# Four weight pieces, eight first taps and one transposition placed elsewhere in a fused attention and MoE kernel

## The chip, the core and the metric

The kernel runs on one core of a Trainium2 chip. A core has five engines that follow their own instruction streams in order: TensorE (PE, matmuls and its weight loads PEld), VectorE (DVE), ScalarE (ACT), GpSimd (POOL) and SyncE (SP), which here issues nearly all transfers between the chip's main memory and SBUF. The metric is the device time of one launch in microseconds.

## The reference, cut to what matters

Attention with rotated q and k (4 batches, 8 heads, 576 tokens, 64 values a head), and behind it a gated layer with a convolution of three taps over the tokens:

```python
scores = scale * np.matmul(rotate(q), rotate(k).transpose(0, 1, 3, 2))
attn = softmax(scores)
x = np.matmul(attn, v)                      # heads side by side: 4 x 576 x 512
h = np.maximum(x @ w_in, 0.0)               # 512 -> 1024
conv_out[:, s] = sum(conv_w[t] * h[:, s + t - 1] for t in range(3))
gate = 1.0 / (1.0 + np.exp(-conv_out))
out = h * gate @ w_out                      # 1024 -> 512
```

## The kernel before

**Steps.** The 32 heads are taken as 16 pairs p, each cut in five row tiles s. One tile is one step, so there are 80 steps n = 5p + s. In a step PE makes the scores of a tile (L261, 4 products in 8 instructions), DVE takes the negated row maxima (L269), ACT the exponentials (L273), and one step later PE turns the result (L321, a leftover part in L358) and ACT copies it to the tile pt (L199). When a pair's five tiles are there, PE multiplies by v in two halves (emit_E, L389), and DVE makes reciprocals of the sums (emit_rinv, L366 to L368), which go by SP through main memory and come back as rb (L371 to L376).

**The second layer.** From step WIDE = 26 on the PSUM pools change and the layer's work is laid into the steps beside attention. Of a block of 288 tokens, unit f (one of eight slices of 128 hidden values) is a call of emit_M1: twelve matmuls (L428), ACT's ReLU into rr (L436), and a chain that is spread over the next steps: conv (DVE: first tap L440, two more taps L442), tanh (ACT, L448), gate (DVE, L451), split (ACT copy L459, then POOL's subtraction L460). The first block's units 0 to 7 are in steps 26, 27, 28, 29, 31, 32, 33 and 34, one each; from step 36 on there are two units in a step, or half a row tile of the second product (L531, from step 37).

**The weights.** They are 64-bit numbers, converted in sixteen pieces of 128 x 512. A piece has five parts: ACT's absolute value into wt (L557), on DVE a clamp (L560), a shift (L566), the low bits (L571) and the result into wf (L576). When the last part is written out the next but one load into w64 is issued on SP (L596). One step later, at rank 0.12, ACT rounds wf into the high half (L626) and POOL subtracts, in four instructions, for the low half (L623). The last four pieces, 12 to 15 in the list (here W0 to W3, the last rows of w_out), live in the pool wl with one buffer of wt and one of wf, and their parts are placed by the table LATEW.

**Order.** The order is written out by hand: `at(n, rank, fn)` puts work in step n at a rank, all engines' streams are filled in rising step and rank, and each engine runs its own stream in that order; only semaphores hold an instruction back. Ranks around the change, from step 26 on: split and tanh 0.1, rounding of a piece 0.12, maxima 0.2, conv and gate of the first block 0.3, the transposition of q or k (emit_TQ, L234 and L237, L243) 0.45, turns 1, exponentials 1.5, copies to pt 1.6, a unit 2, weight parts 2.6, the leftover's copy 5 (11 in step 26), emit_E 10, rotation on POOL (rope, six L190 and three L193) 18, load of v 19, loads of q and k (six transfers each, L149 to L151) 19.6. Raw q and raw k have one buffer each: a load waits for the transposition of the pair before, and the rotation for the load. Pairs that concern us: pair 6 (k transposed in step 28), pair 7 (loads in step 26, rotation in 27 and 28, transposition in 30), pair 8 (loads in step 30, rotation in 32 and 33, transposition in 35).

Of the kernel before, what the change touches and what calls it, by code (L numbers as in the profile page):

```python
# [11 lines left out]
AF = mybir.ActivationFunctionType  # L12
ALU = mybir.AluOpType
# [7 lines left out]
def attention_moe_kernel(ctx, tc, q, k, v, w_in, conv_w, w_out, tab, tabx, out):  # L21
    nc = tc.nc
# [7 lines left out]
    HS = S // 2  # L30
# [5 lines left out]
    scale = float(D) ** -0.5  # L36
# [24 lines left out]
    cw = keep.tile([128, 32], F32, name="cw")  # L61
# [13 lines left out]
    late = {"tail": False, "u": 0}  # L75
# [5 lines left out]
    def defer(k, fn, rank=1):  # L81
        due.setdefault(slot[0] + k, []).append((rank, len(due.get(slot[0] + k, [])), fn))
# [30 lines left out]
    def m_tile():  # L113
        if late["tail"]:
            return psum["t"].tile([128, 512], F32, tag="mt", name="mt")
        ps = m_pair()
        pair["k"] ^= 1
        return ps[1 - pair["k"]]
# [86 lines left out]
    def qk_tiles(p):  # L205
        if p not in QT:
            QT[p] = p2.tile([128, S], F32, tag="qT", name="qT")
            KT[p] = p2.tile([128, S + 64], F32, tag="kT", name="kT")
# [21 lines left out]
    def emit_TQ(p, part):  # L230
        qk_tiles(p)
        x = raw.pop((p, part))[:, :, 0, :]
        if part == "q":
            nc.vector.transpose(out=QT[p].rearrange("p (c i) -> p c i", i=32), in_=x)  # L234
        else:
            kt = KT[p].rearrange("p (c i) -> p c i", i=32)
            nc.vector.transpose(out=kt[:, 2:20], in_=x)  # L237
            if p * STEPS < WIDE:
                for h in range(2):
                    r = slice(64 * h, 64 * h + 64)  # L240
                    nc.vector.transpose(out=krem[p % 2][r, r].rearrange("p (c i) -> p c i", i=32), in_=x[r, 16:18])
            if p * STEPS + STEPS > WIDE:
                nc.vector.transpose(out=kt[:, 0:2], in_=x[:, 16:18])  # L243
# [174 lines left out]
    def emit_M1(blk, f, last=False):  # L418
        b, j = divmod(blk, 2)
        g, rr = late["g"], late["rr"]  # L420
        ps = m_tile()
        fs = slice(128 * f, 128 * f + 128)
        n = 3 * NK
        i = 0
        for kk in range(NK):
            xs = xslot[b, kk, j]
            for w, e in ((winh, 0), (winh, 1), (winl, 0)):
                nc.tensor.matmul(  # L428
                    out=ps[:, 0:XW], lhsT=w[:, kk, fs], rhs=xT[:, xs, e, :], start=(i == 0), stop=(i == n - 1)
                )  # L430
                i += 1
        if f == NF - 1:
            for kk in range(NK):
                free_slots.append(xslot.pop((b, kk, j)))
        r = rr[(blk * NF + f) % len(rr)]
        nc.scalar.activation(out=r[:, 1:XW], in_=ps[:, j:j + XW - 1], func=AF.Relu, scale=0.5)  # L436
        c = late["pc"].tile([128, HS], F32, tag="c", name="c")

        def conv():
            nc.vector.tensor_scalar(out=c, in0=r[:, j:j + HS], scalar1=cw[:, f:f + 1], scalar2=None, op0=ALU.mult)  # L440
            for e in (1, 2):
                nc.vector.scalar_tensor_tensor(  # L442
                    out=c, in0=r[:, j + e:j + e + HS], scalar=cw[:, 8 * e + f:8 * e + f + 1], in1=c,
                    op0=ALU.mult, op1=ALU.add,
                )

        def tanh():
            nc.scalar.activation(out=c, in_=c, func=AF.Tanh)  # L448

        def gate():  # L450
            nc.vector.scalar_tensor_tensor(  # L451
                out=c, in0=c, scalar=1.0, in1=r[:, j + 1:j + 1 + HS], op0=ALU.add, op1=ALU.mult
            )

        def split():
            o = 0
            for dst, n in g_pieces(blk, f):
                hi, lo = dst[:, 0, :], dst[:, 1, :]
                nc.scalar.activation(out=hi, in_=c[:, o:o + n], func=AF.Copy)  # L459
                nc.gpsimd.tensor_tensor(out=lo, in0=c[:, o:o + n], in1=hi.bitcast(F32), op=ALU.subtract)  # L460
                o += n
            ready.add((blk, f))

        if late["tail"]:
            for k, fn in enumerate((conv, tanh, gate, split)):
                defer(k + 1, fn)
        else:
            n = late["n"] + last
            for k, rank, fn in ((0, 0.3 if last else 2.5, conv), (1, 0.1, tanh), (2 - last, 0.3, gate), (3 - last, 0.1, split)):
                at(n + k, rank, fn)  # L470

# [3 lines left out]
    def g_pieces(blk, f):  # L475
        res, tok = [], blk * HS
        end = tok + HS
        while tok < end:
            if tok >= TAIL:
                n = end - tok  # L480
                res.append((late["ga"][:, f, :, tok - TAIL:end - TAIL], n))
            else:
                pos = tok % RING
                k = pos // RA
                n = min(end - tok, (RING if k else RA) - pos, TAIL - tok)
                assert all(t < 0 or t in done_tt for t in ((tok - RING) // 128, (tok + n - 1 - RING) // 128))
                res.append((late["g"][k][:, :, f, pos - RA * k:pos - RA * k + n], n))
            tok += n
        return res
# [178 lines left out]
    for i in range(WEARLY):  # L668
# [3 lines left out]
    WIDE = 26  # L672
# [2 lines left out]
    HALVES = [37, 39, 42, 44, 47, 49, 52, 54, 57, 59, 62, 64, 67, 68, 72, 73, 76, 78]  # L675
    NORM = {4: 8}
    LATEW = (
# [4 lines left out]
    )  # L682
    plan = {}
    onpe = (0, 0.2, 0.5, 1, 2, 2.4, 3, 4, 10)
# [2 lines left out]
    def at(n, rank, fn):  # L687
        plan.setdefault(n, []).append((rank, len(plan.get(n, [])), fn))

    def emit():  # L690
        with tc.manual_schedule(engines=engines):
# [17 lines left out]
            for p in range(1, NP):  # L709
                n = STEPS * p  # L710
                early = n - 10 >= WIDE - 1
                for i, part in enumerate("qk"):
                    if p > 1:
                        at(max(n - 10, WIDE) if early else n - 9 + 2 * i, 19.6 if early else 19, lambda p=p, part=part: load(p, part))
                    at(n - 8 + i if early else max(n - 6 + i, 0) if p > 1 else 0, 18, lambda p=p, part=part: rope(p, part))
                    at(n - 5 if early else max(n - 4 + 2 * i, 2), 0.45, lambda p=p, part=part: emit_TQ(p, part))
                at(n + 1, 19, lambda p=p: load_v(p))
            for p in range(NP):
                n = STEPS * p
# [36 lines left out]
            for n, k in UNITS.items():  # L756
                for i in range(k):
                    blk, f = divmod(late["u"], NF)
                    late["u"] += 1
                    at(n, 2 + 0.4 * i, lambda blk=blk, f=f, last=i == k - 1: emit_M1(blk, f, last))  # L760
# [3 lines left out]
            n = -1  # L764
# [96 lines left out]
```

## Time and profile before

| what | value |
| --- | --- |
| median of 3 runs | 497.78 us (494.35 to 498.48) |
| the profiled execution | 498.89 us, its span 496.9 us |
| mean granted TensorE clock | 0.983 |
| busy PE, PEld | 456.6 us (92%), 360.1 us (72%) |
| busy DVE, ACT, POOL | 364.1 us (73%), 329.2 us (66%), 301.5 us (61%) |
| chain that ended last | PE 69%, DVE 11%, SP's queue 7%, DMA 6%, ACT 4% |

The span runs from the first to the last instruction; 1.99 us of the profiled execution lie outside it. Shares of busy time are means over stages that have different limits, so they are read by stage. In the rows further on, a number in brackets at a row's end is the time for which the engine stood idle in front of it, and behind the arrow stands what ended that wait.

### The profile page before, as it was taken

To read this page: it belongs to the slowest core of one execution; us is meant where nothing else is said; L and a number is where in the kernel's file an instruction comes from. 1 tells how busy PE (TensorE), PEld (TensorE's weight loads), DVE (VectorE), ACT (ScalarE), POOL (GpSimd) and SP (SyncE) were. 2 spreads that over 40 slices of the span, in tenths; PEclk is the share of its full clock that TensorE was granted. 3 is DMA by queue.
4 is the path that set the end of the run, shared out by engine and by line. 5 is a ranking of instruction groups with operands and counts; after the bars stand their busy time and mean duration, and the time that the engine had idled before them with its cause. 6 is when DMAs were issued, how large, how long until landed. Compare 5 with 4: busy or idle time off the path is not lost.

```text
span 496.9 us, 12411 instructions
## 1 busy us (share of the span) xinstructions
PE 456.6 (92%) x4572; PEld 360.1 (72%) x4572; DVE 364.1 (73%) x644; ACT 329.2 (66%) x943; POOL 301.5 (61%) x495
## 2 busy tenths in 40 slices
PE   1869889888687999999999999999999999999997
PEld 1336456555565779797978787979797878899886
DVE  5587897898798988686868687777674665567921
ACT  2678887796476768696868686868687763244510
POOL 3598979999378975848584849393921213234520
PEclk9999989999799899999999999999999999999999
DMA  8986787547542507080807090707120200100011
GB/s 225 149 162 156 152 163 167 116 93 162 114 92 63 82 14 143 14 154 17 151 29 139 14 154 12 141 27 128 41 60 13 60 13 25 42 23 22 0 58 48
DMA packets 140559, 42.71 MB, mean 86 GB/s; under 512 B 132156, under 2 KB 135252, under 8 KB 140500
## 3 DMA queue, kind: packets, MB, share of 16 engines
q1 hardware_dynamic: 139156, 41.54, 40.5%
q8 instruction: 36, 0.59, 0.5%
q10 hardware_dynamic: 1344, 0.39, 0.4%
q14 instruction: 23, 0.19, 0.1%
HBM read 37.12 MB, written 4.79 MB: 84 GB/s over the span
## 4 chain that ended last, share of the span: by engine, by line
PE 69%; DVE 11%; SPq 7%; DMA 6%; ACT 4%; issue 2%; POOL 1%; DVEq 0%; POOLq 0%; ACTq 0%
PE pm L428 13%; PE sp L261 12%; PE pm L531 10%; PE mt L511 10%; PE pm L389 10%; PE mt L428 7%; PE tp L321 5%; SPq L150 3%; DVE negm L269 2%; DMA rk<-k 2%; DVE wt L560 2%; ACT st L273 2%; DMA vm<-v 2%; SPq L151 1%; SPq L149 1%
## 5 line engine op out<-in xcount | busy, mean ns | idle before, releaser
L269 DVE TENSOR_REDUCE negm<-sp 128x1 f32<-128x576 f32 x144 | 102.6, 748 | 36.2 <-PE sp L261 21.9
L273 ACT ACTIVATE st<-sp,negm 128x576 f32<-128x576 f32 x128 | 94.0, 742 | 31.6 <-DVE negm L269 30.8
L261 PE MATMUL sp<-kT,qT 64*128 64x288 f32 (+4 forms) x556 | 103.1, 469 | 5.4 <-ACT st L273 3.0
L199 ACT ACTIVATE pt<-tp 128x512 f32<-128x512 f32 (+3 forms) x176 | 84.1, 530 | 4.8 <-PE tp L321 4.3
L442 DVE SCALAR_TENSOR_TENSOR c<-rr,cw,c 128x288 f32<-128x288 f32 x128 | 79.4, 620 | 4.5
L460 POOL TENSOR_TENSOR gm<-c,gm 128x288 fp32r<-128x288 f32 (+4 forms) x72 | 45.1, 631 | 55.3 <-ACT gm L459 55.1
L428 PE MATMUL pm<-xT,winh 128*128 128x290 f32 x352 | 76.0, 310 | 0.0
L190 POOL TENSOR_TENSOR rq<-rq,tabt 128x192 f32<-128x192 f32 x90 | 59.3, 693 | 17.9 <-DMA rq<-q 17.7
L261 PEld LDWEIGHTS sp<-kT,qT 64*128 64x128 f32 (+1 forms) x556 | 48.1, 179 | 27.5 <-issue 8.8
L410 POOL TENSOR_TENSOR xT<-xn,xT 128x290 fp32r<-128x290 f32 x32 | 28.0, 876 | 59.3 <-ACT xT L406 58.3
L321 PEld LDWEIGHTS tp<-idf,st 64*128 64x128 f32 x1024 | 43.3, 140 | 25.7 <-ACT st L273 15.4
L190 POOL TENSOR_TENSOR rk<-rk,tabt 128x192 f32<-128x192 f32 x90 | 57.4, 671 | 2.9 <-DMA rk<-k 2.9
L428 PEld LDWEIGHTS pm<-xT,winh 128*128 128x128 f32 x352 | 57.4, 193 | 1.9
L321 PE MATMUL tp<-idf,st 64*128 64x64 f32 x1024 | 48.8, 228 | 10.8 <-ACT st L273 10.6
L428 PE MATMUL pm<-xT,winl 128*128 128x290 f32 x176 | 52.7, 299 | 0.0
L389 PE MATMUL pm<-pt,vm 128*64 128x290 f32 x368 | 50.1, 411 | 2.4 <-ACT pt L199 2.4
L531 PE MATMUL pm<-wouth,gm 64*128 64x256 f32 x512 | 49.3, 282 | 0.0
L440 DVE TENSOR_SCALAR c<-rr,cw 128x288 f32<-128x288 f32 x64 | 29.1, 455 | 22.1 <-ACT rr L436 19.3
L451 DVE SCALAR_TENSOR_TENSOR c<-c,rr 128x288 f32<-128x288 f32 x64 | 36.4, 590 | 9.4 <-ACT c L448 9.4
L531 PEld LDWEIGHTS pm<-wouth,gm 64*128 64x128 f32 x512 | 43.0, 185 | 0.0
L389 PEld LDWEIGHTS pm<-pt,vm 128*64 128x64 f32 x368 | 25.8, 136 | 19.8 <-ACT pt L199 3.5
L531 PE MATMUL pm<-woutl,gm 64*128 64x256 f32 x256 | 38.9, 276 | 0.0
(118 smaller groups left out, 909.8 us busy)
## 6 DMA issues: line engine op xcount, KB each, us to landing
rq<-q SPq DMA_DIRECT2D x30, 144.0 KB
rq<-q SPq DMA_DIRECT2D x60, 72.0 KB
rk<-k SPq DMA_DIRECT2D x30, 144.0 KB
rk<-k SPq DMA_DIRECT2D x60, 72.0 KB
w<-moe_w_in SPq DMA_DIRECT2D x8, 512.0 KB
vm<-v SPq DMA_DIRECT2D x32, 128.0 KB
w<-moe_w_out SPq DMA_DIRECT2D x8, 512.0 KB
rb<-rd SPq DMA_DIRECT2D x16, 144.0 KB
```

Source lines behind the costliest of these rows:

```text
L190: nc.gpsimd.tensor_tensor(out=y, in0=y, in1=tabt[:, a:a + 3], op=ALU.mult)
L199: nc.scalar.activation(out=out, in_=in_, func=AF.Copy, scale=1.0 if sc is None else sc)
L261: nc.tensor.matmul(out=out, lhsT=qt[64 * h:64 * h + 64, c], rhs=kt[64 * h:64 * h + 64, a:a + n], start=True, stop=True)
L269: reds.setdefault((p, s), []).append(lambda: nc.vector.tensor_reduce(out=nm, in_=sc, axis=AX.XY if len(sc.shape) == 3 else AX.X, op=ALU.ma ...
L273: lambda: nc.scalar.activation(out=dst, in_=sc, func=AF.Exp, bias=nm, scale=1.0, accum_out=sm)
L321: nc.tensor.transpose(ps[r][:, 64 * k:64 * k + 64], x[i], idf[i, i])
L389: nc.tensor.matmul(out=xp[64 * h:64 * h + 64, :], lhsT=vmain[p][:, h, i, :] if i < 4 else vrem[p % 2][:, h, :], rhs=pt[:, 2 * i + h if i < ...
L428: nc.tensor.matmul(out=ps[:, 0:XW], lhsT=w[:, kk, fs], rhs=xT[:, xs, e, :], start=(i == 0), stop=(i == n - 1))
L442: nc.vector.scalar_tensor_tensor(out=c, in0=r[:, j + e:j + e + HS], scalar=cw[:, 8 * e + f:8 * e + f + 1], in1=c, op0=ALU.mult, op1=ALU.add,)
L460: nc.gpsimd.tensor_tensor(out=lo, in0=c[:, o:o + n], in1=hi.bitcast(F32), op=ALU.subtract)
L511: nc.tensor.matmul(out=ops[tt][:, 0:width], lhsT=g_tile(tt, f, e), rhs=w[:, f, cols], start=(f == 0 and i == 0), stop=(f == NF - 1 and i = ...
L531: nc.tensor.matmul(out=ps[r][:, 0:256], lhsT=g_tile(tt, f, e)[rows], rhs=w[rows, f, cols], start=(f == 0 and i == 0), stop=(f == NF - 1 an ...
```

## The change

Three edits. The first tap of the first block's eight units goes from DVE to ACT and from the step after the unit into the unit's own step (rank 5.2). The table LATEW gets other steps: W0 is cut in halves over steps 26 and 27, W1 over 29 and 31, W2 over 32 and 33, W3 stays whole in 34. The transposition of k of pair 7 goes from step 30 to 31.

```diff
+        def tap():
+            nc.scalar.activation(out=c, in_=r[:, j:j + HS], func=AF.Copy, scale=cw[:, f:f + 1])
+
         def conv():
-            nc.vector.tensor_scalar(out=c, in0=r[:, j:j + HS], scalar1=cw[:, f:f + 1], scalar2=None, op0=ALU.mult)
+            if blk:
+                nc.vector.tensor_scalar(out=c, in0=r[:, j:j + HS], scalar1=cw[:, f:f + 1], scalar2=None, op0=ALU.mult)
             for e in (1, 2):
...
             n = late["n"] + last
+            if not blk:
+                at(late["n"], 5.2, tap)
...
     LATEW = (
-        ((25, 0.4), (26, 2.6), (26, 2.6), (26, 2.6), (26, 2.6)),
-        ((26, 5.5), (27, 2.6), (27, 2.6), (29, 2.6), (29, 2.6)),
-        ((29, 5.5), (31, 2.6), (31, 2.6), (31, 2.6), (31, 2.6)),
-        ((31, 5.5), (33, 2.6), (33, 2.6), (34, 2.6), (34, 2.6)),
+        ((25, 0.4), (26, 2.6), (26, 2.6), (27, 2.6), (27, 2.6)),
+        ((27, 5.5), (29, 2.6), (29, 2.6), (31, 2.6), (31, 2.6)),
+        ((31, 5.5), (32, 2.6), (32, 2.6), (33, 2.6), (33, 2.6)),
+        ((33, 5.5), (34, 2.6), (34, 2.6), (34, 2.6), (34, 2.6)),
     )
...
-                    at(n - 5 if early else max(n - 4 + 2 * i, 2), 0.45, lambda p=p, part=part: emit_TQ(p, part))
+                    at(n - 5 + i * (n - 10 < WIDE) if early else max(n - 4 + 2 * i, 2), 0.45, lambda p=p, part=part: emit_TQ(p, part))
```

## Rows read from the trace of the kernel before

**Rows 1.** The page's slices: PE's busy tenths in 40 slices of the span.

```profile
PE   1869889888687999999999999999999999999997
```

**Rows 2.** Stretches, steps 26 to 30: busy us of each engine, PEclk, DMA share, GB/s.

```profile
117.90:128.10 10.20, 7.08 (x76) 5.08 (x73) 10.06 (x8) 3.20 (x9) 8.07 (x23) 1.00 0.19 64
128.10:135.20 7.10, 5.87 (x30) 4.84 (x32) 3.98 (x9) 5.10 (x15) 2.50 (x4) 0.52 0.88 195
135.20:140.40 5.20, 5.20 (x63) 4.26 (x58) 5.13 (x10) 3.72 (x11) 3.58 (x6) 1.00 0.07 5
140.40:145.40 5.00, 4.87 (x41) 3.23 (x41) 4.83 (x9) 3.04 (x9) 2.45 (x4) 1.00 0.67 121
145.40:153.40 8.00, 6.79 (x64) 4.70 (x61) 6.41 (x13) 5.81 (x16) 7.67 (x12) 1.00 0.22 67
```

**Rows 3.** Timeline of DVE, steps 26 to 34: start, us, instruction, idle before it.

```profile
119.97 6.29 DVE L560 TENSOR_SCALAR wt<-wt 128x512 f32<-128x512 f32 x1
126.75 0.69 DVE L571 SCALAR_TENSOR_TENSOR wt<-w,wt 128x512 int32<-128x512 int32 x1
127.48 0.69 DVE L576 SCALAR_TENSOR_TENSOR wf<-w,wt 128x512 int32<-128x512 int32 x1
...
135.19 1.42 DVE L269 TENSOR_REDUCE negm<-sp 128x1 f32<-128x576 f32 x2 [3.02 <-PE sp L261]
...
136.89 0.71 DVE L440 TENSOR_SCALAR c<-rr,cw 128x288 f32<-128x288 f32 x1
...
151.49 0.78 DVE L237 STREAM_TRANSPOSE kT<-rk 128x576 f32<-128x576 f32 x1 [1.45 <-POOL rk L193]
...
174.41 0.90 DVE L576 SCALAR_TENSOR_TENSOR wf<-w,wt 128x512 int32<-128x512 int32 x1
```

**Rows 4.** DVE's clamp and shift by line: durations in ns, least, median, most.

```profile
L560 DVE TENSOR_SCALAR wt<-wt x17: 404/591/6293, 19.9 to 167.3; 128x512 f32<-128x512 f32 x16, 32x128 f32<-32x128 f32 x1
L566 DVE TENSOR_SCALAR wt<-wt x17: 414/569/1045, 22.3 to 168.2; 128x512 int32<-128x512 int32 x16, 32x128 int32<-32x128 int32 x1
```

**Rows 5.** Timeline of ACT: the wait in step 26, a split, the wait in 35.

```profile
128.21 0.66 ACT L557 ACTIVATE wt<-w 128x512 f32<-128x512 f32 x1 [6.65 <-DVE wf L576]
...
138.94 0.49 ACT L459 ACTIVATE gm<-c 128x288 fp32r<-128x288 f32 x1
...
175.34 0.63 ACT L626 ACTIVATE wouth<-wf 128x512 fp32r<-128x512 f32 x1 [1.50 <-DVE wf L576]
```

**Rows 6.** Timeline of PE: the first work of step 27, and emit_E's second half.

```profile
129.33 0.48 PE L358 MATMUL pm<-idf,st 64*128 64x64 f32 x2 [4.35 <-ACT pt L199]
...
176.35 2.20 PE L389 MATMUL pm<-pt,vm 128*64 128x290 f32 x15 [1.01 <-ACT pt L199]
```

**Rows 7.** Timeline of SP: issues in steps 30 and 31.

```profile
153.54 1.36 SPq L371 DMA_DIRECT2D rd<-rt  x4
...
160.48 0.50 SPq L151 DMA_DIRECT2D rq<-q  x1
...
164.69 0.50 SPq L151 DMA_DIRECT2D rk<-k  x1
```

**Rows 8.** Timeline of POOL: rotations in steps 25, 32 and 33, and what surrounds them.

```profile
120.72 3.35 POOL L190 TENSOR_TENSOR rk<-rk,tabt 128x192 f32<-128x192 f32 x6
124.03 1.68 POOL L193 TENSOR_TENSOR rk<-rk 128x192 f32<-128x192 f32 x3
...
160.71 2.40 POOL L623 TENSOR_TENSOR woutl<-wf,wouth 128x128 fp32r<-128x128 f32 x4
163.76 4.08 POOL L190 TENSOR_TENSOR rq<-rq,tabt 128x192 f32<-128x192 f32 x6 [0.65 <-DMA rq<-q]
...
170.81 4.95 POOL L190 TENSOR_TENSOR rk<-rk,tabt 128x192 f32<-128x192 f32 x6
175.72 1.90 POOL L193 TENSOR_TENSOR rk<-rk 128x192 f32<-128x192 f32 x3
177.58 0.86 POOL L460 TENSOR_TENSOR gm<-c,gm 128x288 fp32r<-128x288 f32 x1
```

## The prediction, made before the changed kernel ran

> **What bounds the kernel now.** I read the page's slices first: from about the fifteenth slice on PE shows nines nearly to the end, before that sixes to eights [rows 1]. So a microsecond saved in the later steps off PE is worth nothing, and one by which PE's unbroken stretch starts sooner is worth a whole one. The change lies just ahead of that stretch, in steps 26 to 36, and the question is when PE gets its first work after which it never waits again. The timeline of PE gives that point: the second half of emit_E in step 35, at 176.35, for which it stood idle 1.01 us [rows 6]. That wait ends with a copy by ACT, which stood behind the rounding L626 of the last weight piece W3, which waited for DVE's L576 of W3, started at 174.41 [rows 3, 5]. So **the start of L576 of W3 sets the end of this stage**, and I follow how it gets there.
>
> Then I read the stretches by step. In steps 28 and 29 DVE is busy 5.13 of 5.20 and 4.83 of 5.00 us; it is the bound there [rows 2]. Steps 26, 27 and 30 are longer for other reasons. In step 26 (10.20 us) one clamp of W0 took 6.29 us where the median is 0.59 [rows 3, 4]; meanwhile POOL rotated k of pair 6 without a pause, 120.72 to 125.7 [rows 8]. In step 27 (7.10 us) DVE is busy 3.98 us and waits 3.02 for scores [rows 2, 3]: ACT had stood 6.65 us in front of L557 of W1, which needs the buffer that L576 of W0 reads [rows 5]; with ACT's copies held, PE was idle 4.35 us [rows 6], and after that it ran at a granted clock of 0.52 in the stretch, the lower of its two levels, 1.2 instead of 2.4 GHz [rows 2]. In step 30 (8.00 us) DVE waits 1.45 us at the transposition of k of pair 7 for POOL's rotation [rows 2, 3].
>
> **The change, step 26 to step 30.** Up to the clamp in step 26 all streams are the same, so I keep its 6.29 us. Behind it L571 and L576 of W0, 0.69 us each [rows 3], go to step 27: 1.4 us gained. In step 27 L557 of W1 now stands at the very end, so ACT's copies in step 26 are free, PE goes on without the 4.35 us and without the slow clock. What then sets step 27 is DVE: 3.98, less a tap of some 0.7 (0.71 one step later) and less the clamp and shift of W1 (medians 0.59 and 0.57), plus 1.38, is 3.5 [rows 2, 3, 4]; ACT has as much to do, so I take 4.0 of the 7.10: 3.1 gained. If PE gives its slow clock to these steps all the same, this falls to some 1. Step 28 loses the tap: 0.7. Step 29 loses the tap and exchanges two parts of a piece for two others; but PE was busy 4.87 of its 5.00 us [rows 2], so I count 0.4, not 0.9. In step 30 DVE's 6.41 lose the tap, 0.7, and the 0.78 of k's transposition, and the wait of 1.45 goes: some 4.9. PE's 6.79 of that step [rows 2] are a limit only so far as PE has not begun ahead of DVE, and it has, since maxima wait for nothing there; I take 5.0 of 8.00, 3.0 gained (1.2, if PE's 6.79 rule). Sum at the end of step 30: 1.4 + 3.1 + 0.7 + 0.4 + 3.0 = **8.6 us**, with 5 to 9 as ends.
>
> The tap itself costs ACT eight instructions like the split's copy of the same shape, 0.49 us at most [rows 5], before some overlap; 0.4 a step. ACT has gaps of over a microsecond in each step (busy 3.04 of 5.00, 3.72 of 5.20, 5.81 of 8.00 [rows 2]). If they were full it would cost up to 0.49 a step, 3.9 in all; it is held in the ends. It needs no wait but the ReLU ahead of it on the same engine. The transposition of k in step 31 lets the load of raw k of pair 8, issued in step 30, start only then; on SP the next behind it are the load of W3 and v. The rotation needs that k late, so this costs nothing.
>
> **The change, step 31 to step 35.** Here an order turns round. wf has one buffer. L576 of W3 may write it only when POOL's four L623 of W2 have read it. Before, W2 was finished in step 31, its L623 ran at 160.71, ahead of POOL's two rotations of pair 8 [rows 8]. Now W2 is finished in step 33 and its L623 are in POOL's stream in step 34, behind both rotations (steps 32 and 33) and behind one L460. And the rotations can't start sooner than raw q of pair 8 has landed, which SP loads only after the reciprocals' trip of step 30. I count from the issue of that trip, 153.54 before [rows 7]: to the rotation's start at 163.76 it is 10.2 us (the last load of q is issued at 160.48); from there to the start of the second rotation at 170.81 7.05; the second took 6.77, to 177.58 [rows 8]. When DVE stands still a rotation takes 3.35 + 1.68 = 5.03 [rows 8]; DVE will stand still in its last third, so 6.1. L460 0.85. The L623 took 2.40 with DVE at work [rows 8], 2.0 by the same ratio as L190 (3.35 to 4.08). L576 itself 0.69 [rows 3]. Together 26.9 us. Before, L576 of W3 ended at 174.41 + 0.90, that is 21.8 after the trip's issue. So **5.1 of the 8.6 us are given back to a new wait of DVE for POOL**, and 3.5 are left. Behind the waiting L576 on DVE stand the maxima of step 35, and on ACT L626 of W3 and the copies that emit_E needs. The bounds: both rotations at 5.03 gives 2.8 given back; both at the slowest rows (4.95 + 1.90) and L623 at 2.40 gives 6.1 [rows 8].
>
> That wait has a second price. PE can do the first half of emit_E, but then idles several microseconds before the second. After 4.35 us of idling its granted clock was 0.52 over 7.10 us, with PE busy 5.87 [rows 2, 6]. There it cost little beyond the step; here every later microsecond of PE counts, so a spell like it would cost up to 2.9 (half of 5.87). It can also fall into the idle time itself, and cost nothing. I take 2.0. Net gain 3.5 - 2.0 = 1.5. The profiled execution took 498.89, so 497.4; the median run lies 1.1 below the profiled one, so **496.3 us**.
>
> W3's load is now behind the twelve loads of pair 8 on SP, whose last is issued 11.2 us after the trip (164.69) [rows 7]. W3's first part on ACT comes at about 15 us after it; if the piece lands later, ACT and DVE wait, but DVE waits for POOL then anyway, so nothing is added up to some 4 us of lateness.
>
> **The rivals.** (a) *The wait on POOL is short and PE keeps its clock*: rotations near 5.03, gain 8.6 - 2.8 = 5.8, **492.0**. For it: fewer taps on DVE beside the rotations; against: DVE works through the whole first rotation. (b) *No wait on POOL at all*, the whole 8.6: **489.2**. It would take q landing 3 us sooner or more; no row shows that. (c) *The clamp's 6.29 us do not come again*. Then DVE's maxima of step 27 can begin at 125 (PE ended there, 129.33 - 4.35) instead of 126.7, 1.8 sooner: **494.5** [rows 3, 6]. For it: only one of 17 clamps shows it [rows 4]; against: nothing ahead of it is changed. The Trainium skill, page "SBUF — State Buffer", section "SBUF: two separate sides", says that VectorE and GpSimd share a port pair as an exclusive lock, held for one instruction by whichever starts first. By that the clamp would wait for one POOL instruction, some 0.6 us, and this rival would be the rule; the trace does not agree, since the 6.29 us span all nine instructions of a rotation. (d) *The gain of the first steps does not come*: PE's 6.79 rule step 30, slow clock in steps 27 and 28, taps fill ACT: 8.6 becomes 5, less 5.1, no further clock price: **497.9**, no change. (e) *Slower*: one more clamp is caught by a rotation as that of step 26 was. W3's clamp now stands in step 34, beside the second rotation, and W1's in step 29 beside that of pair 7's k. One costs 6.29 - 0.59 = 5.7 us of DVE where DVE rules: **502.0**. It decides from a stall of 1.5 us on.
>
> **How the numbers follow.** The forecast 0.42 (own range 494 to 498.5), (a) 0.16, (b) 0.07, (c) 0.13, (d) 0.14, (e) 0.08. About one per cent, 5 us, is what a measurement of this kernel tells from no change. Below 492.8 are (b), most of (a), a little of (c): 0.20. Above 502.8 is part of (e) and a little of (d): 0.05. Within: 0.75. The range 490.5 to 501.0 leaves out (b), most of (e) and the ends of the others.
>
> **What would show each step right or wrong.** In the changed profile: L557 of W1 no longer with a wait of over 6 us, PE's idle time ahead of step 27 gone, and a granted clock of 1.0 from 128 to 135; the reciprocals of step 30 end near 145; no wait at k's transposition of pair 7. Then L576 of W3 on DVE with a wait of 3 to 6 us for POOL's L623, PE idle 3 us or more ahead of emit_E's second half, near 172.9, and a stretch at about half clock behind it. If that L576 has no wait, (b) holds. If the clamp of step 26 is short, (c). If the reciprocals end after 149, the first sum is wrong. A clamp of over 2 us in steps 29 to 34 is (e).

## The result, and the profile after

The changed kernel takes 499.81 us, median of its runs (497.61 to 508.68); the kernel before, timed beside it on the same chip, takes 496.44 us (492.88 to 502.08). The ratio is 1.0077, with a 95% interval of 1.0047 to 1.0106: it is slower by 0.8%. The ratios here and below are formed from the fast runs alone, those within 1.5% of the fastest of their kernel, so they are not the quotients of the medians beside them, and of a kernel with two lengths a part of the longer executions is left out (12 of 29 where the kernel before has a median of 497.89). The forecast was 496.3 us, a little under the median of 497.78 that was known for the kernel before. The time lies within the range of 490.5 to 501.0 and within the 1% that was called no change, but the small effect has the other sign.

| | before | after |
|---|---|---|
| median, us | 496.44 | 499.81 |
| profiled execution, us | 498.89 | 500.04 |
| its span, us | 496.9 | 498.2 |

In the changed file the lines behind the new function stand six lower: the tap on ACT is L440, the conversion's clamp L566, its result L582, the rounding L632, POOL's subtraction L629, the zeros at the borders of rr L784 and L785.

I go through the profile by the points that the prediction named. First the stretches of steps 26 to 30, which answer to [rows 2]; the columns are the same: busy us of PE, PEld, DVE, ACT and POOL, the granted clock as a share of 2.4 GHz, DMA share, GB/s.

```profile
120.67:128.78 8.11, 7.05 (x76) 5.05 (x71) 8.07 (x5) 4.03 (x13) 7.45 (x22) 1.00 0.31 78
128.78:132.42 3.64, 3.50 (x30) 3.13 (x32) 3.57 (x7) 3.06 (x11) 0.00 (x0) 1.00 0.89 156
132.42:137.52 5.10, 4.41 (x55) 3.27 (x50) 4.94 (x9) 5.10 (x16) 4.24 (x7) 1.00 0.00 0
137.52:142.12 4.60, 4.60 (x45) 3.77 (x43) 4.29 (x8) 4.60 (x15) 4.36 (x7) 1.00 0.86 160
142.12:147.36 5.24, 5.24 (x50) 3.14 (x48) 4.74 (x10) 4.20 (x13) 4.38 (x7) 1.00 0.20 77
...
172.90:179.70 6.80, 3.53 (x15) 3.27 (x17) 5.81 (x9) 3.30 (x9) 5.01 (x9) 0.52 0.01 2
```

Steps 26 to 30 together take 26.69 us instead of 35.50. The clock is full in all five of them, as forecast. The last row is behind them: from 172.9 on PE runs at the lower level, 1.2 GHz, which the trace of before does not show there. The timeline of DVE (start, us, instruction, the idle time before it and its releaser) tells why:

```profile
120.67 1.42 DVE L269 TENSOR_REDUCE negm<-sp 128x1 f32<-128x576 f32 x2 [1.87 <-PE sp L261]
...
122.70 5.71 DVE L566 TENSOR_SCALAR wt<-wt 128x512 f32<-128x512 f32 x1
...
147.36 1.42 DVE L269 TENSOR_REDUCE negm<-sp 128x1 f32<-128x576 f32 x2 [0.40 <-PE sp L261]
...
149.64 0.76 DVE L237 STREAM_TRANSPOSE kT<-rk 128x576 f32<-128x576 f32 x1
...
173.85 1.27 DVE L582 SCALAR_TENSOR_TENSOR wf<-w,wt 128x512 int32<-128x512 int32 x1 [4.52 <-POOL woutl L629]
...
201.22 1.42 DVE L269 TENSOR_REDUCE negm<-sp 128x1 f32<-128x576 f32 x2
```

L582 of W3 waits 4.52 us for POOL's L629 of W2. On POOL these four stand behind both rotations of pair 8, as the order by steps and ranks puts them:

```profile
157.30 4.13 POOL L190 TENSOR_TENSOR rq<-rq,tabt 128x192 f32<-128x192 f32 x6
161.39 2.81 POOL L193 TENSOR_TENSOR rq<-rq 128x192 f32<-128x192 f32 x3
...
164.94 4.85 POOL L190 TENSOR_TENSOR rk<-rk,tabt 128x192 f32<-128x192 f32 x6
169.75 1.67 POOL L193 TENSOR_TENSOR rk<-rk 128x192 f32<-128x192 f32 x3
171.39 0.78 POOL L464 TENSOR_TENSOR gm<-c,gm 128x288 fp32r<-128x288 f32 x1
172.14 1.68 POOL L629 TENSOR_TENSOR woutl<-wf,wouth 128x128 fp32r<-128x128 f32 x4
```

And in PE's timeline the second half of emit_E, which answers to the last of [rows 6], begins after 5.56 us of idling and takes 4.16 us where it took 2.20:

```profile
176.17 4.16 PE L389 MATMUL pm<-pt,vm 128*64 128x290 f32 x16 [5.56 <-ACT pt L199]
```

So the chain that the prediction wrote down is there link by link. Measured against the trace of before it also comes out in size: from the maxima of step 26 to those of step 40 the changed kernel takes 201.22 - 120.67 = 80.55 us. The kernel before took 199.93 - 117.93 = 82.00, by the same line in its timeline of DVE:

```profile
117.93 1.42 DVE L269 TENSOR_REDUCE negm<-sp 128x1 f32<-128x576 f32 x2 [1.86 <-PE sp L261]
...
153.43 1.38 DVE L269 TENSOR_REDUCE negm<-sp 128x1 f32<-128x576 f32 x2
...
199.93 1.42 DVE L269 TENSOR_REDUCE negm<-sp 128x1 f32<-128x576 f32 x2
```

That is 1.45 us less, and 1.5 had been forecast. Yet the median rose. The experiments therefore had two questions: is the trace of before a fair sample of the kernel before, and which part of the change costs what.

In the tables below "26 to 31", "31 to 40" and "26 to 40" are stretches between the starts of the maxima (L269 on DVE) of those steps. Behind step 40 the traces of this case take 297.0 to 297.8 us, whatever the kernel.

### The profile page after: what moved, and what is told of

Its sections match the earlier page's. It is cut to its first block, busy times and chain, and to the rows that moved or that the text cites. A ratio compares the mean times of both kernels' runs of the same rounds, so it can differ in the third digit from the quotient of the medians.

```text
span 498.2 us, 12409 instructions
## 1 busy us (share of the span) xinstructions
PE 456.1 (92%) x4572; PEld 361.6 (73%) x4572; DVE 361.5 (73%) x636; ACT 331.9 (67%) x951; POOL 302.5 (61%) x495
## 4 chain that ended last, share of the span: by engine, by line
PE 66%; DVE 9%; POOL 6%; ACT 6%; DMA 5%; SPq 4%; issue 3%; DVEq 0%; POOLq 0%; ACTq 0%
PE pm L428 12%; PE sp L261 11%; PE pm L537 10%; PE mt L517 10%; PE pm L389 10%; PE mt L428 7%; PE tp L321 5%; ACT st L273 2%; DVE negm L269 2%; POOL rk L190 2%; DMA w<-moe_w_in 2%; DVE wt L566 2%; POOL rq L190 2%; ACT pt L199 1%; DMA rq<-q 1%
## 5 line engine op out<-in xcount | busy, mean ns | idle before, releaser
L269 DVE TENSOR_REDUCE negm<-sp 128x1 f32<-128x576 f32 x144 | 102.7, 749 | 40.4 <-PE sp L261 25.0
L261 PE MATMUL sp<-kT,qT 64*128 64x288 f32 (+4 forms) x556 | 101.4, 466 | 4.7 <-ACT st L273 2.3
L446 DVE SCALAR_TENSOR_TENSOR c<-rr,cw,c 128x288 f32<-128x288 f32 x128 | 80.6, 630 | 4.2
L428 PE MATMUL pm<-xT,winh 128*128 128x290 f32 x352 | 74.7, 306 | 0.0
L410 POOL TENSOR_TENSOR xT<-xn,xT 128x290 fp32r<-128x290 f32 x32 | 28.4, 887 | 63.1 <-ACT xT L406 63.0
L428 PEld LDWEIGHTS pm<-xT,winh 128*128 128x128 f32 x352 | 56.4, 189 | 1.8
L190 POOL TENSOR_TENSOR rk<-rk,tabt 128x192 f32<-128x192 f32 x90 | 56.4, 659 | 1.1 <-DVE negm L269 1.1
L389 PE MATMUL pm<-pt,vm 128*64 128x290 f32 x368 | 51.5, 422 | 5.7 <-ACT pt L199 5.7
L455 DVE SCALAR_TENSOR_TENSOR c<-c,rr 128x288 f32<-128x288 f32 x64 | 37.4, 605 | 9.9 <-ACT c L452 9.8
L389 PEld LDWEIGHTS pm<-pt,vm 128*64 128x64 f32 x368 | 27.4, 140 | 22.7 <-ACT pt L199 6.4
L444 DVE TENSOR_SCALAR c<-rr,cw 128x288 f32<-128x288 f32 x56 | 22.9, 408 | 20.6 <-ACT rr L436 20.0
```

Source lines behind the costliest of these rows:

```text
L190: nc.gpsimd.tensor_tensor(out=y, in0=y, in1=tabt[:, a:a + 3], op=ALU.mult)
L261: nc.tensor.matmul(out=out, lhsT=qt[64 * h:64 * h + 64, c], rhs=kt[64 * h:64 * h + 64, a:a + n], start=True, stop=True)
L269: reds.setdefault((p, s), []).append(lambda: nc.vector.tensor_reduce(out=nm, in_=sc, axis=AX.XY if len(sc.shape) == 3 else AX.X, op=ALU.ma ...
L389: nc.tensor.matmul(out=xp[64 * h:64 * h + 64, :], lhsT=vmain[p][:, h, i, :] if i < 4 else vrem[p % 2][:, h, :], rhs=pt[:, 2 * i + h if i < ...
L428: nc.tensor.matmul(out=ps[:, 0:XW], lhsT=w[:, kk, fs], rhs=xT[:, xs, e, :], start=(i == 0), stop=(i == n - 1))
L446: nc.vector.scalar_tensor_tensor(out=c, in0=r[:, j + e:j + e + HS], scalar=cw[:, 8 * e + f:8 * e + f + 1], in1=c, op0=ALU.mult, op1=ALU.add,)
```

## The experiments

### The kernel before once more

No edit: a second look at the same program.

> The kernel before once more, for a second trace of it. Theory A (the order on POOL: the changed kernel loses by DVE's wait in step 34 for POOL's subtraction of W2, and by TensorE's slow clock behind it) expects nothing new. Theory B (the trace of before that the prediction was made from was one of its longer executions: the clamp of 6.29 us, or the slow clock of step 27, is not in most of them, and what the change removes there was mostly not there) expects a clamp under 1 us in step 26 or a granted clock above 0.9 in step 27, and a span of 491 to 494 us. If the clamp takes some 6 us again and the clock is near 0.5 again, B falls.

Measured: 493.54 us, span 491.8, on a chip where the kernel before had a median of 495.66. Its timeline of DVE:

```profile
118.81 1.42 DVE L269 TENSOR_REDUCE negm<-sp 128x1 f32<-128x576 f32 x2 [1.86 <-PE sp L261]
...
120.84 1.06 DVE L560 TENSOR_SCALAR wt<-wt 128x512 f32<-128x512 f32 x1
...
148.42 1.38 DVE L269 TENSOR_REDUCE negm<-sp 128x1 f32<-128x576 f32 x2
...
169.24 0.90 DVE L576 SCALAR_TENSOR_TENSOR wf<-w,wt 128x512 int32<-128x512 int32 x1
...
194.75 1.42 DVE L269 TENSOR_REDUCE negm<-sp 128x1 f32<-128x576 f32 x2
```

The clamp of W0 took 1.06 us, not 6.29 [rows 3]. ACT's wait in front of L557 of W1, 6.65 us in [rows 5], is down to 2.23, by the timeline of ACT:

```profile
124.67 0.68 ACT L557 ACTIVATE wt<-w 128x512 f32<-128x512 f32 x1 [2.23 <-DVE wf L576]
```

And PE's granted clock, 0.52 behind that wait in [rows 2], is full in the stretch from 128 to 135 (columns as above):

```profile
128.00:135.00 7.00, 5.91 (x66) 4.52 (x66) 6.83 (x14) 5.27 (x17) 3.94 (x12) 1.00 0.65 109
```

Steps 26 to 30 take 29.61 us instead of 35.50, and 26 to 40 takes 75.94 instead of 82.00. What follows: the same program has two lengths some 6 us apart in this region. Of the 8.8 us that the change saves there against the first trace, 5.9 (35.50 - 29.61) are a delay that this execution of the kernel before does not have; 2.9 (29.61 - 26.69) are left.

### The rotation of k of pair 6 moved away from that clamp

The kernel before, with that rotation on POOL in step 27 instead of 25, behind the conversion of W0:

```diff
-  at(n - 8 + i if early else max(n - 6 + i, 0) if p > 1 else 0, 18, ...)
+  at(n - 8 + i if early else max(n - 6 + i + 2 * i * (p == 6), 0) if p > 1 else 0, 18, ...)
```

> The kernel before with POOL's rotation of k of pair 6 in step 27, behind the subtraction of W0, instead of in step 25: the clamp of W0 in step 26 then meets no rotation, and the zeros of rr come earlier. Theory B (executions differ by whether that clamp is caught for 6 us) expects that the longer half of the executions goes: highest time under 498 us, ratio to before 0.990 to 0.997, a clamp of 0.4 to 0.7 us. If the spread stays at 492 to 501 us, it comes from elsewhere.

Measured: 494.06 us (493.44 to 496.34) against 497.22 (492.91 to 502.54), ratio 0.9964 (0.9931 to 0.9997). In its trace 26 to 40 takes 76.05 us. The clamp, from the timeline of DVE:

```profile
120.83 0.78 DVE L560 TENSOR_SCALAR wt<-wt 128x512 f32<-128x512 f32 x1
```

What follows: with the rotation elsewhere the upper half of the kernel's times is gone. The times of the kernel before on that chip fall into two heaps, one from 492.9 to 496.3 and one from 497.2 to 502.5, about half of the runs in each; all runs of this variant lie in the span of the lower heap. So the meeting of clamp and rotation makes the second length, and here not only semaphores held an instruction back. In the two traces in which the clamp was held (119.97 + 6.29 = 126.26 before, 122.70 + 5.71 = 128.41 after) it ended some 0.55 us behind POOL's last instruction of that rotation (125.71, 127.85 by the timelines of POOL). In nine other traces with the rotation in that place it took 0.42 to 1.06 us. In one of these (the variant with only the rotation of k of pair 8 moved, below) it began at 122.53, within the rotation that runs from 122.14 to 127.51, and still took 0.49 us. The Trainium skill, page "SBUF — State Buffer", section "SBUF: two separate sides", says that a GpSimd instruction and a VectorE instruction that runs in a two-port mode or has two inputs in SBUF lock a shared port pair, and that whichever starts first keeps it for that whole instruction. By that the clamp, if it is such an instruction, should wait for one instruction of POOL, some 0.6 us. The 0.42 to 1.06 us agree with it, the two held clamps do not. The moment at which the clamp begins does not tell them apart either. Counted from the start of POOL's L410 ahead of the rotation it began after 0.03 us in the first trace (held) and 0.04 in the second (1.06 us long), after 0.61 in the changed kernel (held) and 0.60 and 0.59 in the two variants with added matmuls below (0.49 us long each). What decides which of the two happens stays open.

### The table alone

The kernel before with only the new LATEW (the table in the diff above).

> The kernel before with the new table of the weight pieces alone. Theory A expects the whole loss and more: L576 of W3 waits 4 us or more for POOL, k of pair 7 is waited for in step 30, ratio to before 1.007 to 1.02. Theory C (the taps on ScalarE lengthen the way from scores to exponentials) expects 0.99 to 1.00.

Measured: 503.02 us (501.76 to 504.52) against 495.66, ratio 1.0138 (1.0084 to 1.0192). Two waits, the first in the timeline of DVE:

```profile
177.56 1.27 DVE L576 SCALAR_TENSOR_TENSOR wf<-w,wt 128x512 int32<-128x512 int32 x1 [5.07 <-POOL woutl L623]
```

The second in that of ACT:

```profile
165.75 0.68 ACT L557 ACTIVATE wt<-w 128x512 f32<-128x512 f32 x1 [2.19 <-DMA w<-moe_w_out]
```

And three stretches in which PE ran at the lower clock:

```profile
151.60:158.40 6.80, 6.80 (x40) 6.01 (x40) 6.15 (x11) 5.90 (x16) 3.25 (x6) 0.53 0.58 124
168.70:175.50 6.80, 6.79 (x36) 4.05 (x36) 3.69 (x5) 2.12 (x7) 6.80 (x11) 0.53 0.00 0
178.90:185.70 6.80, 5.83 (x24) 4.54 (x26) 5.40 (x12) 3.70 (x11) 2.57 (x5) 0.53 0.02 4
```

What follows: the table by itself is the loss, and by its trace (85.87 us from step 26 to 40) a larger one than the whole change; the intervals of the two ratios overlap a little. It brings the wait for POOL; it also makes W3's load late for ACT, 2.19 us (1.30 in the changed kernel, at 163.51), which the prediction had allowed for as covered.

### The transposition of k alone

The kernel before with only the last edit of the change (k of pair 7 in step 31).

> The kernel before with the transposition of k of pair 7 in step 31, alone. It takes away a wait of DVE of 0.35 to 1.45 us in step 30. TensorE, which has the two halves of emit_E there, ended 2 us ahead of it, so 0 to 1.5 us less are expected, ratio 0.997 to 1.000; over 1.002 would mean that the load of k of pair 8, which then starts a step later, is late for its rotation.

Measured: 498.2 us (494.39 to 503.01) against 497.89, ratio 1.0031 (0.999 to 1.0072). Its trace is one without the held clamp, 76.85 us from step 26 to 40 against 75.94. What follows: no effect that can be told from none. The wait that it removes, 1.45 us in [rows 3], is 0.35 in the second trace of the kernel before; there was little to win. A ratio over 1.002 had been taken beforehand as a sign that the load of k of pair 8 comes late; in this trace no rotation waits for a load of k, so that is not what the 1.0031 shows.

### The change without the table

The changed kernel with the LATEW of before: the taps and the transposition are left.

> The changed kernel with the old table: taps on ScalarE and the later transposition, nothing else. Theory A expects no wait for POOL in step 34 and a ratio to before of 0.990 to 0.998. Theory C expects the loss here, 1.004 or more.

Measured: 495.98 us (494.33 to 497.82) against 495.66, ratio 1.0003 (0.9969 to 1.0038). From step 26 to 40 it takes 78.43 us: 31.23 in 26 to 31 and 47.20 in 31 to 40, against 29.61 and 46.33 in the second trace of the kernel before. No wait for POOL at W3. Instead, in the timeline of ACT:

```profile
129.65 0.53 ACT L440 ACTIVATE c<-rr,cw 128x288 f32<-128x288 f32 x1 [5.45 <-POOL rr L784]
```

In that of PE:

```profile
131.21 0.48 PE L358 MATMUL pm<-idf,st 64*128 64x64 f32 x2 [3.58 <-ACT pt L199]
```

And in the stretch behind it:

```profile
130.60:137.40 6.80, 6.19 (x32) 5.13 (x34) 1.68 (x5) 5.00 (x16) 4.13 (x9) 0.50 0.49 82
```

What follows: the moved tap has a wait that I had denied. It reads rr with the zeros at its borders. POOL writes these zeros behind the rotation of k of pair 6. On ACT the copies for PE stand behind the tap, so PE idles 3.58 us, and its clock falls to 1.2 GHz. While the tap was DVE's and a step later, this cost less: DVE waits 1.11 us for the same zeros in the second trace of the kernel before, and not at all in the first, where the held clamp kept it. In the changed kernel, in the timeline of ACT, the wait is 3.63 us:

```profile
127.92 0.54 ACT L440 ACTIVATE c<-rr,cw 128x288 f32<-128x288 f32 x1 [3.63 <-POOL rr L784]
```

### The zeros set by DVE

The variant without the table, with the zeros on DVE, placed in step 26 at rank 2.5:

```diff
-  nc.gpsimd.memset(t[:, 0:1], 0.0)
-  nc.gpsimd.memset(t[:, XW:XW + 1], 0.0)
+  at(n, 2.5, lambda t=t: nc.vector.memset(t[:, 0:1], 0.0))
+  at(n, 2.5, lambda t=t: nc.vector.memset(t[:, XW:XW + 1], 0.0))
```

> Taps on ScalarE and the later transposition with the old table of the pieces, and the zeros of rr set by VectorE. Theory D expects that the wait of 5.45 us at the first tap, TensorE's idle 3.6 us and its slow clock behind it go, and 3 to 5 us less than the same kernel with POOL's zeros: ratio to before 0.990 to 0.995. Theory C (the taps by themselves fill ScalarE) expects 1.000 still.

Measured: 495.71 us (489.51 to 498.32) against 497.22, ratio 0.994 (0.9888 to 0.9992). In its trace 26 to 40 takes 73.12 us, and the tap waits for nothing, by the timeline of ACT:

```profile
124.33 0.54 ACT L440 ACTIVATE c<-rr,cw 128x288 f32<-128x288 f32 x1
```

What follows: without the wait the taps on ACT are worth something, 75.94 - 73.12 = 2.8 us in the region. The mean of all twelve times lies 0.4% below that of the kernel before. But the times now fall into two heaps again, four from 489.5 to 492.9 and eight from 495.1 to 498.3. That is what a held clamp that is no longer covered by the tap's wait would do; this variant's one trace is of the lower heap (clamp 0.90), so the upper one was not seen.

### Only POOL's order undone

The changed kernel with the rotation of k of pair 8 one step later, in 34, so that POOL's four L629 of W2 come first:

```diff
-  at(n - 8 + i if early else ..., 18, ...)
+  at(n - 8 + i + i * (p == 8) if early else ..., 18, ...)
```

> The changed kernel with POOL's rotation of k of pair 8 in step 34 instead of 33, so that the subtraction of W2 stands ahead of it on POOL. Theory A expects DVE's wait in step 34 to go from 4.5 us to under 1, no idle time of over 2 us on TensorE ahead of emit_E's second half, no slow clock there, and 5 to 6 us less than the changed kernel: ratio to before 0.993 to 0.999. If A is only a part (B), 2 to 4 us less than the changed kernel.

Measured: 493.8 us (492.29 to 496.98) against 495.66, ratio 0.995 (0.991 to 0.999). The place of the wait, first in the timeline of POOL:

```profile
165.45 2.49 POOL L629 TENSOR_TENSOR woutl<-wf,wouth 128x128 fp32r<-128x128 f32 x4
...
169.12 4.43 POOL L190 TENSOR_TENSOR rk<-rk,tabt 128x192 f32<-128x192 f32 x6
```

In that of DVE:

```profile
168.63 1.07 DVE L582 SCALAR_TENSOR_TENSOR wf<-w,wt 128x512 int32<-128x512 int32 x1
...
175.24 0.78 DVE L237 STREAM_TRANSPOSE kT<-rk 128x576 f32<-128x576 f32 x1 [1.45 <-POOL rk L193]
```

In that of PE:

```profile
170.75 2.20 PE L389 MATMUL pm<-pt,vm 128*64 128x290 f32 x15 [1.22 <-ACT pt L199]
```

The maxima of steps 26, 31 and 40:

```profile
120.50 1.42 DVE L269 TENSOR_REDUCE negm<-sp 128x1 f32<-128x576 f32 x2 [1.87 <-PE sp L261]
...
146.59 1.38 DVE L269 TENSOR_REDUCE negm<-sp 128x1 f32<-128x576 f32 x2
...
194.73 1.42 DVE L269 TENSOR_REDUCE negm<-sp 128x1 f32<-128x576 f32 x2
```

And in the stretch around the wait:

```profile
165.00:175.00 10.00, 8.38 (x76) 5.35 (x77) 8.52 (x12) 7.30 (x22) 10.00 (x15) 1.00 0.01 2
```

What follows: with this one edit of the order the wait is gone, the clock stays full, and 26 to 40 takes 74.23 us instead of 80.55. The kernel comes out below the kernel before. Of these 6.3 us, 5.7 lie behind step 31 (53.86 - 48.14) and are the price of POOL's order, wait and clock together; 0.6 lie ahead of it, where the edit changes nothing and this trace has no held clamp. The rest of the change is worth 75.94 - 74.23 = 1.7 us against the shorter trace of the kernel before. The edit's own cost is the 1.45 us for which DVE now waits at k's transposition.

### The same, with the zeros on DVE

Both edits above in the changed kernel.

> The changed kernel with POOL's rotation of k of pair 8 in step 34, and the eight border columns of rr set to zero by VectorE in step 26 instead of by POOL, where they stand behind the rotation of k of pair 6. Theory D (the tap on ScalarE waits for those zeros, and what is behind it on ScalarE waits with it) expects the tap's wait of 3.5 us in step 26 gone, no idle time of TensorE ahead of step 27, and 0.5 to 2 us less than with the rotation moved alone: ratio to before 0.990 to 0.994. If only the order of W2's subtraction counts (A), 0.995 as without it.

Measured: 492.77 us (491.64 to 496.38) against 497.22, ratio 0.9939 (0.9906 to 0.9972); 26 to 40 takes 73.81 us, 0.4 less than with the zeros on POOL (74.23). What follows: where W0 is cut in halves, the tap's wait was nearly covered. The two ratios, 0.995 and 0.9939, can't be told apart.

### The clock's price by itself: matmuls in the gap

The changed kernel with unread matmuls ahead of emit_E's second half, so that PE stays busy while DVE waits for POOL; 26 of them here. The trace shows each as two instructions, and the lines behind them stand four lower:

```diff
+        if (p, j) == (6, 0):
+            warm = psum["m"] and m_pair()[0][0:64, 320:512]
+            for k in range(26):
+                nc.tensor.matmul(out=warm, lhsT=vmain[p][:, 0, 0, :], rhs=pt[:, 0, 0:192], start=True, stop=True)
```

> The changed kernel with 26 more matmuls on TensorE in step 35, between the two halves of emit_E, whose results nobody reads; they fill most of the 5.6 us for which TensorE waits there. The wait for POOL stays. If the slow clock behind the wait costs by itself, as the prediction had it (2.0 us), the second half of emit_E takes 2.9 us instead of 4.9, and the kernel 1.5 to 2.5 us less than the changed one: ratio to before 1.003 to 1.005. If the slow clock is hidden behind other engines at that place: 1.0077 as the changed one. If the extra matmuls run longer than the wait, 1.008 or more.

Measured: 501.06 us (498.03 to 505.91) against 497.22, ratio 1.0093 (1.0053 to 1.0134). Inconclusive: they take 8.45 us and run past the end of the wait, so they delay what they were to help. The timeline of PE:

```profile
168.43 8.45 PE L399 MATMUL pm<-pt,vm 128*64 128x192 f32 x51
```

Its trace has one use all the same: the clamp of W0 was not held there, and steps 26 to 30 take 26.41 us, beside 26.69 in the changed kernel with a held clamp; the next variant, not held either, takes 26.44. So a held clamp seems to cost the changed kernel next to nothing (three traces): ACT and PE stand behind the tap's wait until nearly the same time anyway.

### Fourteen instead of 26

The same edit with range(14).

> The changed kernel with 14 instead of 26 more matmuls between the two halves of emit_E in step 35 (results unread). The 26 took 8.45 us, longer than the wait that they were to fill; 14 should take 4.5 us, inside the 5.6. If the slow clock behind the wait costs by itself: granted clock 1.0 in the second half, which then takes 2.9 us, and 1 to 2.5 us less than the changed kernel, ratio to before 1.003 to 1.006. If it is hidden: 1.0077 as the changed kernel.

Measured: 498.09 us (496.08 to 501.82) against 497.89, ratio 1.0068 (1.0031 to 1.0105). The timeline of PE:

```profile
173.50 4.71 PE L399 MATMUL pm<-pt,vm 128*64 128x192 f32 x28
179.68 2.20 PE L389 MATMUL pm<-pt,vm 128*64 128x290 f32 x15 [1.46 <-ACT pt L199]
```

That of DVE:

```profile
177.36 1.27 DVE L586 SCALAR_TENSOR_TENSOR wf<-w,wt 128x512 int32<-128x512 int32 x1 [4.53 <-POOL woutl L633]
...
188.95 1.42 DVE L269 TENSOR_REDUCE negm<-sp 128x1 f32<-128x576 f32 x2 [0.85 <-PE sp L261]
```

And the stretch behind them:

```profile
176.00:190.00 14.00, 12.54 (x122) 10.02 (x122) 10.59 (x20) 8.89 (x25) 7.02 (x12) 1.00 0.12 31
```

What follows: the wait is the same, 4.53 us, but PE keeps the full clock. From the result of W3's conversion to the maxima of step 37 it takes 188.95 - 177.36 = 11.59 us; in the changed kernel it takes 187.16 - 173.85 = 13.31. So the slow clock costs 1.7 us in the trace. From step 31 to 40 only 0.7 of it is left (53.18 against 53.86), since in this trace the conversion of W3 comes 1.0 us later behind the maxima of step 31. I had expected a ratio of 1.003 to 1.006, a miss; in the timed runs 1.0068 and 1.0077 can't be told apart.

### Without the table, and with the other rotation moved

The variant without the table, with the rotation of k of pair 6 in step 27 (the edit shown above). That frees the clamp and lets POOL write the zeros early.

> Taps on ScalarE and the later transposition of k of pair 7, the old table of the pieces, and POOL's rotation of k of pair 6 in step 27 behind the subtraction of W0. Theories B and D together (the clamp of step 26 meets no rotation, the zeros of rr stand ahead of it) expect both the long executions and the tap's wait to go: ratio to before 0.985 to 0.991, highest time under 495 us, 3 us or more less than the kernel before with the same rotation moved (0.9964), which would be the worth of taps and transposition. If the taps are worth nothing by themselves: 0.996.

Measured: 492.52 us (490.58 to 495.53) against 497.89, ratio 0.9936 (0.9898 to 0.9973). The tap at 123.44 waits for nothing, 26 to 40 takes 73.88 us, and the times no longer fall into two heaps. What follows: both waits in step 26 came from that one rotation on POOL, the held clamp and the late zeros. Against the kernel before with the same rotation moved, taps and transposition are worth 76.05 - 73.88 = 2.2 us in the traces; the ratios, 0.9936 and 0.9964, have intervals that overlap. I had expected 0.985 to 0.991 and no time over 495 us, a miss.

### A table of halves that keeps POOL's order

The variant just above, with W2 in halves over steps 31 and 32; W3's first part, on ACT, goes from step 31 to 32 with it:

```diff
-        ((29, 5.5), (31, 2.6), (31, 2.6), (31, 2.6), (31, 2.6)),
-        ((31, 5.5), (33, 2.6), (33, 2.6), (34, 2.6), (34, 2.6)),
+        ((29, 5.5), (31, 2.6), (31, 2.6), (32, 2.6), (32, 2.6)),
+        ((32, 5.5), (33, 2.6), (33, 2.6), (34, 2.6), (34, 2.6)),
```

> Taps on ScalarE, the later transposition, POOL's rotation of k of pair 6 in step 27, and a third table of the pieces: W0, W1 and W3 on VectorE as in the kernel before, W2 in halves over steps 31 and 32. W2's subtraction on POOL is then in step 33, ahead of the rotation of k of pair 8, so no wait for it is expected in step 34 (by theory A: under 1 us). With the old table the piece W2, whole in step 31, left TensorE idle 3.2 us ahead of step 33; the halves should take 1 to 2 us of that: ratio to before 0.988 to 0.992. If the halves bring nothing: 0.9936 as with the old table.

Measured: 491.96 us (489.09 to 495.28) against 495.5, ratio 0.9934 (0.9903 to 0.9964). L582 of W3 waits 0.35 us for POOL, against 4.52 in the changed kernel:

```profile
163.53 1.28 DVE L582 SCALAR_TENSOR_TENSOR wf<-w,wt 128x512 int32<-128x512 int32 x1 [0.35 <-POOL woutl L629]
```

This has the lowest ratio of the kernels here, 0.7% below the kernel before, but the halves add nothing that can be measured to the variant without them (0.9936); I had expected 0.988 to 0.992, a miss.

## Why the prediction was wrong, step by step

The stage lengths beside each other, in us; all are differences of starts in DVE's timelines:

| kernel | 26 to 31 | 31 to 40 | 26 to 40 | ratio to before |
|---|---|---|---|---|
| before, first trace (clamp held) | 35.50 | 46.50 | 82.00 | 1 |
| before, second trace | 29.61 | 46.33 | 75.94 | 1 |
| changed | 26.69 | 53.86 | 80.55 | 1.0077 |
| table alone | 30.11 | 55.76 | 85.87 | 1.0138 |
| changed without the table | 31.23 | 47.20 | 78.43 | 1.0003 |
| changed, k of pair 8 rotated later | 26.09 | 48.14 | 74.23 | 0.995 |

- **What bounds the kernel** was right for both kernels: L582 of W3 sets where PE's unbroken work begins. In ten of the 14 traces PE waits 0.25 to 5.56 us ahead of emit_E's second half. It is no law: in the changed kernel without the table PE's last wait, 3.57 us at 161.39, ends twelve us ahead of L582 of W3 (173.73).
- **Steps 26 to 30, 8.6 us**: 8.8 were measured against the trace that the sum was made from. Of the terms, step 27 was forecast at 4.0 us and took 3.64, step 30 at 5.0 and took 5.24, step 29 at 0.4 less and took 0.4 less. Steps 26 and 28 were off in opposite ways: step 26 lost 2.0 instead of 1.4, step 28 0.1 instead of 0.7. The reciprocals of step 30 ended at 146.96 and not "near 145": step 26 had begun 2.7 us later (120.67 against 117.93).
- **The tap "needs no wait but the ReLU"** was wrong. It waited 3.63 us for the zeros. In this sum the mistake cost nothing, because the clamp held DVE until 128.41 anyway; without the table and without the held clamp it cost about what the taps bring (78.43 against 73.12 us from step 26 to 40; the ratios, 1.0003 and 0.994, have intervals that overlap a little).
- **Steps 31 to 35, the order turned round**: right in kind. From the trip's issue to the end of L582 of W3 I had counted 26.9 us; it took 175.12 - 146.99 = 28.1. Before it had taken 21.8; in the second trace of the kernel before it takes 21.6 (148.53 to 170.14). So 6.3 to 6.5 us are given back, not 5.1: mis-sized by 1.2 to 1.4, a little above the upper bound of 6.1. By terms: the first rotation's start to the second's took 7.64 instead of 7.05, the second 6.45 instead of 6.1, L582 itself 1.27 instead of 0.69; the L629 took 0.3 less. That upper bound left out POOL's L410 between the two rotations (0.81 us at 170.04 before), which the lower bound of 2.8 needs to come out; with it that bound is 6.9.
- **The slow clock, 2.0 us**: right in place (172.9 to 179.7) and nearly in size, 1.7 by the filled gap.
- **The step that failed is the last: "the median run lies 1.1 below the profiled one".** It took the trace of before as an execution like the others and its gap to the median as an offset that the changed kernel would keep. In fact the kernel before runs in two lengths, and the profiled execution was one of the long ones. Of my first sum of 8.6 us, some 5.9 was a delay that only these have, most of it in steps 26 and 27. The change removes it where it is; where it isn't, only 2.9 is gained and 7.5 (53.86 - 46.33) lost, 4.6 net. With about half of the runs in each heap, the region alone gives (4.6 - 1.4)/2 = 1.6 us slower. The medians say 3.4, the means 4.0.
- **What is missing** may lie ahead of step 26, where nothing is changed: that part takes 117.9 to 119.8 us in the five traces of the kernel before and its variants, and 120.5 to 120.7 in five of the nine of the changed one and its variants, the others from 117.0 to 123.4. The spread there is older than the change's steps. The maxima that begin at 41.29 in the first trace of the kernel before begin at 43.89 in the changed one, and at 41.3 to 46.5 over the 14 traces; from them to the maxima of step 26 all take 75.4 to 77.5. Some 7 us ahead of them ACT waits for a load of w_in, 2.24 us before and 3.29 after (by the timelines of ACT, to 34.12 and 35.17), and PE's granted clock from 38 to 50 us is 1.00 before and 0.86 after. Over the 14 traces that clock lies between 0.72 and 1.00, and both kernels' variants have traces near 0.86 and at 1.00. So the first 50 us seem to hold a second matter of chance; whether the change has a part in it, so few traces don't settle.
- **What could have shown it:** the three times given with the kernel before were 494.35, 497.78 and 498.48, and the 6.29 us clamp stood alone among 17. I kept it "since nothing ahead of it is changed". That holds for a program's order, not for a race between two engines.

The rivals. (a) and (b), a short wait or none, are out: 4.52 us. (c), the clamp not held, had the right doubt and the wrong sum: it priced what a free clamp would give the changed kernel, 1.8 us (126.7 - 125 is 1.7), where the trace without a held clamp shows 0.3 (26.69 against 26.41). It left out that a free clamp makes the kernel before some 6 us faster, so that the change loses. (d), the first gain not coming, was nearest in its outcome, but for none of its reasons: there was no slow clock in steps 27 and 28, and step 30 wasn't held by PE's 6.79 us. (e), another held clamp in steps 29 to 34, did not happen: the clamps there took 0.67 to 0.81 us.

Left open are what decides whether the clamp is held, and whether the longer first 26 steps are chance; by them some 2 of the 3.4 to 4.0 us are unexplained. Giving wf a second buffer would take away the wait for POOL without moving anything; it wasn't tried.

## What to carry to other kernels

A stall that stands alone in a trace (one of 17 like instructions ten times as long) has to be treated as a matter of chance until a second trace or the spread of the times says otherwise; two heaps in the times mean two baselines, and a change is summed against each. When work is moved by steps, write down each engine's stream behind it: a buffer with one copy turns "two steps later" into a wait for whatever the reading engine has queued ahead. And an operation moved to another engine and an earlier step inherits all writers of its operand, even the two columns of zeros.

## What the runs showed of the hardware

A VectorE clamp that else takes 0.42 to 1.06 us was held for 5.71 and 6.29 us beside a rotation of nine back-to-back GpSimd instructions in two of eleven traces, and not in the others. With the rotation elsewhere the spread of the kernel's times fell from 9.6 us (492.91 to 502.54, 35 runs) to 2.9 (493.44 to 496.34, 12 runs).

An idle time of 5.56 us on PE was followed by a stretch at 0.52 of the full clock, and one of 3.58 us by a stretch at 0.50; one of 1.46 us was not (1.00). The stretch behind the first cost 1.7 us beyond the wait itself.
